# Laying out anew the places of attention steps, q loads and GpSimd sums between the matmul groups of a linear-attention + FFN kernel

## The chip, the cores and the metric

One core of one Trainium2 chip runs the whole program. The time is device microseconds (us) of one execution, lower is better. Engines: PE (TensorE, matmuls), DVE (VectorE), ACT (ScalarE), POOL (GpSimd), and SP, from whose queue nearly all transfers are issued. Each engine runs its own instructions in program order and waits for the others by semaphores.

## The reference

```python
q_s = exp(q - max(q, axis=-1)); q_s /= sum(q_s, axis=-1) + 1e-9     # 8 batches, 8 heads, 576 x 64
k_s = exp(k - max(k, axis=2));  k_s /= sum(k_s, axis=2) + 1e-9      # softmax over the sequence
kv = einsum('bhsd,bhse->bhde', k_s, v)
attn = einsum('bhsd,bhde->bhse', q_s, kv)
x = attn.transpose(0, 2, 1, 3).reshape(4608, 512)
h = x @ w_in                                                        # 512 -> 2048
g = maximum(h, 0) + log1p(exp(-abs(h)))                             # softplus
out = g @ w_out                                                     # 2048 -> 512
```

## The kernel before

The 4608 tokens go in 9 tiles of 512. For each tile the attention gives x (512 tokens x 512), then 16 chunks of the 2048 hidden columns follow, each with an up group of matmuls (x by a chunk of w_in), a softplus, and a down group (by a chunk of w_out). Every f32 product of the FFN is three matmuls on high and low parts (hi/lo, hi/hi, lo/hi). Attention for tile t+1 or later is prepared while the FFN of tile t runs, so PE always has FFN matmuls, and the small attention matmuls (to PSUM tiles `att`) are put between their groups.

The instruction order of every engine is the order of the Python calls, and that order is written out by hand in tables of step names. Tile 0 follows a table `FIRST` that ends at about 119.6 us and is untouched. Tiles 1 and 2 follow `SINGLE`, 32 rows, called **places 0 to 31** here: tile 1 is places 0 to 15, tile 2 is 16 to 31. One row is `before|middle|after`, and the loop runs

```python
ph = up(t, j, cs)                                # 12 matmuls, L758 to L760
before, middle, after = SINGLE[NJ * (t - 1) + place].split("|")
run(before, ops)
split_soft()                                     # g_hi on ACT (L772), g_lo on DVE (L773), for the place before
soft = n, softplus(ph, cs)                       # ACT, L766
run(middle, ops)
while pending and pending[0][0] <= n - 2:
    i, g = pending.pop(0)
    down(*order[i], g)                           # 12 matmuls of two places back, L793 to L795
run(after, ops)
```

Tiles 3 to 8 go in three pairs (3 and 4, 5 and 6, 7 and 8) by `PAIRS[s]`. Each pair has 32 rows `before|after` in which 12, 12, 6 and 12 up matmuls (L1118) come ahead of `before` and 5, 4, 10 and 5 down matmuls (L1138) between `before` and `after`, and then 16 or 18 rows with 12 down matmuls each. Row r of pair s is called P0.0, P0.1 and so on.

The names in a row are steps. A leading digit is the tile that is prepared (in `PAIRS`, `a` and `b` are the two tiles of the next pair). What each step issues:

- `2u30` to `2u35`: the kv product of head pair 3 for tile 2. 0: maximum of k (DVE L418) and its all-reduce over partitions (POOL L420); 2: subtract it (DVE L435); 3: exp in place (ACT L443); 4: reciprocal of the sums (DVE L458, L459); 5: split into hi and lo, ACT L477, ACT L478, DVE L479, twice, one waiting for the other. `2u3*` is the place where the 10 matmuls for it (L448) and the load of a later k/v tile (L375, L376) stand.
- `2x30` to `2x33`: 0 flips softmaxed q into PSUM (DVE L661), 1 stacks its hi and lo parts (ACT L666, DVE L668), `2x3*` is the place of its matmuls (L674), 2 adds the two results (ACT L683, L684, DVE L690, L691), 3 splits x for the FFN. One of these and one `u` share the two PSUM banks `att0` and `att1`.
- `2q0` to `2q11`: softmax of q in halves: 0, 1 maximum (DVE L567), 2 join, 3, 4 subtract (DVE L573), 5, 6 exp (ACT L576), 7, 8 sums (DVE L579), 9 invert, 10, 11 multiply (DVE L587). `2Q0`, `2Q1` load the two halves of q of tile 3 (SP, L542).
- `s40` to `s43`: sums of w_in chunks for the pairs, sum 4 of 8. 0: two additions on POOL (L974), 1: four additions on POOL (L977 to L980), 2: an ACT copy (L984) and a POOL subtraction (L985), 3: the stores (SP). `p4` stores parts (SP), `d0` rearranges kv (ACT, DVE), `h0` splits a chunk of weights.
- `f0` to `f10`: the x operands of the pair by splits (ACT L1006, DVE L1007) and subtractions (DVE L1012); `U`, `D` load weights for the pairs.
- `S2.4`, `J2.4`, `L2.4`, `g1.4`, `G3` in the pairs: ACT copy of a PSUM bank (L1189), DVE addition (L1192), softplus (ACT L1195), and g_hi/g_lo as above.

A softplus and an exp need different tables on ACT; each change of the kind costs an `ACT_TABLE_LOAD`, which stands ahead of the instruction that needs it.

Of the kernel before, what the change touches and what calls it, by code (L numbers as in the profile page):

```python
# [44 lines left out]
SINGLE = [
    "|2u00 2q1 2u10 2u02|",
    "|2u12 2u03 p1 2q0 2q2 h0 2u13 2q4|",
    "2u0* 2q6 2q3 2q8 2u1*|h1|2u20",
    "|2u04 2u30 2u14 2u05 2u15|",
    "s00 p0 2u22 2u32||2q5 2u33",  # L50
    "2q7 2q9 2u23|2u2* 2d0 2u24 2u3* 2q10|2u25 2x00",
    "|s01 2q11|2d1 2u34 2x01 2u35 s02",
    "s03 2d2 2x0* 2x02||2x03 2d3 2x10 2x11 s10",
    "||2x1*",
    "2x12|s11 2x13 s12 p3|s13",
    "2x20 2x21 2x2* 2x22|2x23|2x30",
    "3u00 3u10 2x31||3u12 2Q0",
    "2Q1 3u02 2x3* 2x32 3q1||2x33",
    "3q0 3q2 p2 3u03 3u13 3u0* 3u1* 3u14 3q4 3u04 p4|3q3 3u15|3q5 3u20 3q6 3u30 3u32",
    "||",  # L60
    "3q8 3q7 s20 3u22|3u05 3q9 3u33 3q10 3u23|",
    "3u2* 3u24 3u3*||",
    "3u25 s21 3u34 3x00 3x01|s22 3q11|",
    "3u35|3x0* s23 3x02 3x10|3x11 3Q0",
    "s30 s40 s31||3x1* s50 p7 3x12",
    "3x20 s41||s51",
    "s42 3x21|3x2*|s32 3x22 3x30 s43 s52 3Q1 3x31",
    "4q1||",
    "3x3* 4u00|3x32 4u10 p5 4u02|4u12 4u03",
    "4u13 4u0* 4q0|4u1*|",  # L70
    "s53 p6 4q2 4u04 4q3 4q4 4u20 4u14 4u30 4u22 4q5 4q6|4u32 s33 s60 4u05 4q7 4u33|4q8 4u15 4u23 4q9",
    "||4u2* 4u24 4u3* 4q10 4u34 U0 4u25",
    "4x00|4u35|4x01",
    "4x0* f1 4x02 s70 4x10|s71|",
    "U1 4x11 s72 4q11 4x1* 4x12 4x20||4x21 s61 f0",
    "4x2*||s73 4x22 4x30 s62",
    "s63 4x31|U2 D1 4x3*|4Q0 4Q1 f2 4x32 D0 D2 f4",
]
PAIRS = [
    [  # L80
        "f5 f3 f6 S1.0 J1.0|",
        "|f8 f7 f10 S2.0",
        "au00 f9 S3.0|J3.0",
        "au02 L1.0 J2.0 au10 L4.0 g1.0|aq1 au12",
        "|au03 S1.1 J1.1",
        "|S2.1 au13",
        "L1.1 aq0 au0* aq2 aq4 S3.1 g4.0 au1*|J3.1",
        "|g1.1 aq6 L4.1 L3.0 au14 J2.1",
        "aq3|g4.1 S1.2 J1.2 aq5 au20",
        "|S2.2 L1.2",  # L90
        "au30|au22 S3.2 J3.2",
        "aq7|aq8 au15 aq9 J2.2 L4.2",
        "au04 L3.1 au32 g1.2 g4.2 S1.3 au05 J1.3|",
        "au23 aq10 au2* S2.3 au33 au3* aq11 au24 au34|L1.3 au25 L2.1",
        "S3.3 ax00 J3.3|",
        "ax01 au35 g1.3|J2.3 L4.3 ax0* bu00",
        "ax02 S1.4 ax10|J1.4",
        "|L1.4 aQ0 g4.3 ax11 S2.4 ax1*",
        "ax12|S3.4 J3.4 ax20 g1.4",
        "J2.4 bq0 ax21 L4.4|bu10",  # L100
        "S1.5 J1.5|ax2* L2.0 ax22",
        "L2.2 ax30 g4.4 S2.5 bu02|aQ1",
        "|ax31 S3.5 J3.5 L1.5 ax3* L2.4",
        "bu12 bq1 bq2 bu13 J2.5 L4.5|g1.5 L3.4 bq4 ax32",
        "bu03|S1.6 bu0* g4.5 J1.6 bu1*",
        "bq6|S2.6",
        "bu20 L2.3 bq3 L3.2 bu04|S3.6 L1.6 bu14 J3.6",
        "J2.6|L4.6 g1.6",
        "bq8 S1.7 bu22 bu30|bu23 J1.7 bu32 bq5",
        "|S2.7 bq7 g4.6 bq9",  # L110
        "bu05 bu15 bu33|bu2* S3.7 bu24 J3.7 bq10 bu3*",
        "L1.7 g1.7 bu25 bq11 L3.7 bx00 L4.7 bu34 J2.7|L2.5",
        "g4.7 bx01|G0 bu35",
        "|G1",
        "bx0*|bx02",
        "G2 bx10 L3.6|",
        "nf1|bx11 L3.3 G3 bx1*",
        "G4 nf0|",
        "bx12 bx20 G5|",
        "bx21|bx2*",  # L120
        "nf2 L2.6 L2.7 G6 G7 bx22 L3.5|G8 bx30 bx31",
# [2 lines left out]
        "nf4 G10 bx3*|",
        "bx32|",
        "bQ1 G11 nf5|bQ0 nf3 G12",
        "|nf6 G13 nf8 nf10",
        "nf9 G14 nf7|G15",
    ],
    [  # L130
        "aq0 S1.0|J1.0 aq1 L1.0",
        "S2.0|",
        "S3.0 J3.0|au00",
        "L4.0 au10 au02 J2.0 g1.0|au12 au03",
        "S1.1 J1.1 au13|",
        "g4.0 L1.1 S2.1|",
        "S3.1 aq2 J3.1|",
        "au0* aq3 au1*|J2.1 L3.0 aq4 g1.1 L4.1",
        "S1.2 J1.2 aq6|au14 aq5 au20 g4.1",
        "|au30 S2.2",  # L140
        "|S3.2 au22 J3.2 au23 L2.0",
        "|L4.2 J2.2 L1.2",
        "g1.2 au15 au32 L3.1 S1.3 au33 aq7 aq8 J1.3|au04",
        "|S2.3 au05 g4.2",
        "S3.3 aq9 au2* au3*|aq11 J3.3 bu00 L2.1",
        "L1.3 au34 au24 aq10 au25|g1.3 L4.3 J2.3",
        "bu10 bu12|ax00 au35 g4.3 ax01 ax0* S1.4 J1.4 ax02",
        "ax10 L1.4 S2.4|ax11",
        "S3.4|aQ0 J3.4 bu02 ax1* g1.4",
        "ax12 ax20 bu03 J2.4 L4.4|L2.3",  # L150
        "|ax21 ax2* S1.5 g4.4 J1.5",
        "ax22 bq0 ax30 aQ1|S2.5",
        "ax31|bu13 S3.5 J3.5 ax3* ax32 L1.5 bu0* bq1",
        "|J2.5 L2.4 bu1* bu04 L4.5",
        "bu20 bq2 g1.5 S1.6 bu05 L3.3 bu30|bu32 bq4 bq6 bu22 J1.6",
        "|S2.6 g4.5 L3.4",
        "|S3.6 J3.6 bu14",
        "J2.6|L1.6 g1.6 L4.6",
        "bq3 bu23|L2.5 S1.7 bq8 bu33 g4.6 bq5 J1.7",
        "S2.7 bq7 bu15|bu2* nf0 bq9 bu24 L1.7",  # L160
        "|bu3* bu25 S3.7 J3.7",
        "bq10 bu34 bq11 g1.7 bx00 bu35 J2.7 L4.7|",
        "bx01 g4.7|G0",
        "bx0*|",
        "G1 bx02 L3.2|bx10",
# [1 line left out]
        "|bx11 L3.5",
        "L2.2 G3 bx1* L2.7|bx12",
        "G4 bx20|G5 nf1",
        "bx21|G6 bx2*",  # L170
        "|",
        "G7 bx22 bx30 L3.6 G8|",
        "bQ1 bx31 nf2 G9 nf4|bx3*",
        "bx32|",
        "G10|nf5 L3.7 L2.6 G11",
        "G12 nf6 nf10|",
        "G13 nf3|",
        "G14 nf8|bQ0 nf7 nf9 G15",
    ],
    [  # L180
        "S1.0 J1.0|L1.0",
        "|S2.0",
# [1 line left out]
        "L4.0 J2.0|",
        "g1.0 g4.0 S1.1|J1.1",
        "|S2.1 L1.1",
        "S3.1 J3.1|",
        "L4.1 g1.1|J2.1",
        "S1.2 J1.2|",
        "L1.2|g4.1 S2.2",  # L190
        "S3.2|J3.2",
        "J2.2|L4.2 g1.2",
        "S1.3|J1.3",
        "|S2.3",
        "g4.2 L2.0|S3.3 J3.3",
        "J2.3 L1.3|L3.0 L4.3",
        "g1.3|L2.1 S1.4 J1.4 g4.3",
        "S2.4|",
        "S3.4 J3.4 L1.4|L3.4",
        "|L4.4 J2.4",  # L200
        "g1.4 g4.4|L3.1 S1.5 J1.5 L1.5 L3.3",
        "|S2.5 L3.2",
        "L2.2 S3.5|J3.5",
        "|g1.5 J2.5 L4.5 g4.5",
        "S1.6|J1.6",
        "S2.6|",
        "S3.6 J3.6|",
        "L4.6 L1.6 L2.3 J2.6 g1.6|",
        "S1.7 J1.7 g4.6|",
        "|L2.4 S2.7",  # L210
        "L1.7|S3.7 g1.7 J3.7",
        "|L3.5 L4.7 J2.7",
        "L2.5 g4.7 L2.6|",
        "G0|L2.7",
        "|G1",
        "|G2 G3",
# [1056 lines left out]
```

## Time and profile before

| | |
|---|---|
| median of 3 runs | 853.41 us (851.46 to 854.73) |
| the profiled execution | 854.46 us: its span 852.7 us, and 1.8 us around it |
| mean granted TensorE clock of the span | 0.992 of full |
| busy, share of the span | PE 97%, DVE 64%, ACT 61%, POOL 14% |
| tile 0 (untouched) | 0 to 119.6 us |
| tiles 1 and 2 (`SINGLE`) | 119.6 to 333 us |
| the first two pairs (`PAIRS[0]`, `PAIRS[1]`) | 333 to 646 us |
| the last pair (`PAIRS[2]`) | 646 to 852.7 us |

The profile is of one execution. An engine is busy where it executes; where the text says that an instruction waited, the trace has idle time of its engine just ahead of it and names what ended that time. The granted clock is the share of TensorE's full clock that the chip allowed in a stretch.

### The profile page before, as it was taken

The numbers are of one execution on the slowest core, as the hardware profiler recorded it, in microseconds if no ns is written. First come the engines' busy times: TensorE is split into PE (matmuls) and PEld (weight loads), VectorE is DVE, ScalarE is ACT, GpSimd is POOL, SyncE is SP. The second block draws the span as 40 slices with busy tenths as digits, with TensorE's granted clock in tenths as the row PEclk, the third lists the DMA queues.
The fourth block names the chain that finished last, engine by engine and source line by source line (L and its number), as shares of the span: only waits on it lengthen the run. The fifth ranks groups of instructions, "written<-read, shape, count | busy, mean of one in ns | idle before, by whom it ended". The sixth has DMA issues, their size and how long they took to land.

```text
span 852.7 us, 11505 instructions
## 1 busy us (share of the span) xinstructions
PE 823.4 (97%) x4172; PEld 673.4 (79%) x4172; DVE 543.0 (64%) x849; ACT 519.1 (61%) x861; POOL 115.8 (14%) x203
## 2 busy tenths in 40 slices
...
GB/s 344 371 367 45 40 136 192 81 185 185 126 220 153 269 161 320 216 222 250 169 259 229 236 240 221 202 209 184 198 211 251 174 231 170 232 175 178 119 233 100
DMA packets 79896, 172.72 MB, mean 203 GB/s; under 512 B 5088, under 2 KB 51936, under 8 KB 70624
## 3 DMA queue, kind: packets, MB, share of 16 engines
...
q8 instruction: 33, 0.54, 0.3%
...
## 4 chain that ended last, share of the span: by engine, by line
PE 75%; DVE 9%; ACT 7%; issue 4%; DMA 3%; POOL 2%; SPq 0%; DVEq 0%; ACTq 0%; POOLq 0%
PE po L1138 29%; PE ph L1118 24%; PE ph L758 3%; PE ph L759 3%; PE ph L760 3%; PE po L793 3%; PE po L795 3%; PE po L794 3%; DMA kvt<-in_kv_tail 2%; PE att L674 2%; PE att L448 1%; DVE q L587 1%; DVE g_lo L773 1%; DVE two L668 1%; ACT two L666 1%
## 5 line engine op out<-in xcount | busy, mean ns | idle before, releaser
L1138 PE MATMUL po<-w,g_hi 128*128 128x512 f32 x784 | 246.0, 390 | 0.0
L1118 PE MATMUL ph<-w,w 128*128 128x512 f32 x864 | 213.6, 391 | 0.9 <-ACT x L1189 0.5
L1118 PEld LDWEIGHTS ph<-w,w 128*128 128x128 f32 x864 | 161.0, 188 | 36.2 <-DVE w L1192 1.6
L1138 PEld LDWEIGHTS po<-w,g_hi 128*128 128x128 f32 x784 | 146.7, 188 | 30.4
L1138 PE MATMUL po<-w,g_lo 128*128 128x512 f32 x392 | 152.8, 390 | 0.5 <-DVE g_lo L773 0.5
L1192 DVE TENSOR_TENSOR w<-ph,w 128x512 f32<-128x512 f32 x54 | 37.2, 689 | 90.7 <-PE ph L1118 47.9
L773 DVE TENSOR_TENSOR g_lo<-w,g_hi 128x512 fp32r<-128x512 f32 x77 | 52.8, 690 | 56.3 <-ACT g_hi L772 52.5
L1138 PEld LDWEIGHTS po<-w,g_lo 128*128 128x128 f32 x392 | 73.6, 188 | 16.3 <-DVE g_lo L773 0.9
L772 ACT CAST g_hi<-w 128x512 fp32r<-128x512 f32 x77 | 47.4, 618 | 47.4 <-PE po L1138 45.9
L1189 ACT COPY w<-ph 128x512 f32<-128x512 f32 x54 | 31.7, 587 | 72.9 <-PE ph L1118 72.6
L793 PE MATMUL po<-w,g_hi 128*128 128x512 f32 x164 | 65.3, 398 | 0.0
L795 PE MATMUL po<-w,g_lo 128*128 128x512 f32 x164 | 64.9, 396 | 0.0
L794 PE MATMUL po<-w,g_hi 128*128 128x512 f32 x164 | 64.9, 396 | 0.0
L420 POOL PARTITION_ALL_REDUCE mb<-mx x28 | 28.1, 1003 | 256.5 <-DVE mx L418 236.8
L758 PE MATMUL ph<-x,w 128*128 128x512 f32 x142 | 56.9, 400 | 0.0
L759 PE MATMUL ph<-x,w 128*128 128x512 f32 x142 | 55.5, 391 | 0.0
L760 PE MATMUL ph<-x,w 128*128 128x512 f32 x142 | 55.4, 390 | 0.0
L668 DVE TENSOR_TENSOR two<-att,two 64x512 fp32r<-64x512 f32 x56 | 38.6, 689 | 22.8 <-ACT two L666 22.1
L666 ACT CAST two<-att 64x512 fp32r<-64x512 f32 x56 | 32.6, 581 | 21.9 <-DVE att L661 21.2
L418 DVE TENSOR_REDUCE mx<-kvt 128x128 f32<-128x640 f32 x28 | 36.9, 1329 | 9.9 <-DMA kvt<-in_kv_tail 9.8
L766 ACT ACTIVATE l<-ph 128x512 f32<-128x512 f32 (+1 forms) x50 | 29.1, 581 | 14.9 <-PE ph L760 13.6
L773 DVE TENSOR_TENSOR g_lo<-l,g_hi 128x512 fp32r<-128x512 f32 x46 | 34.1, 741 | 4.8 <-ACT g_hi L772 4.0
...
## 6 DMA issues: line engine op xcount, KB each, us to landing
...
```

Of the source, the lines that this page charges most:

```text
L666: nc.scalar.copy(w[zs, z], ps[zs])
L668: nc.vector.tensor_tensor(out=w[SIDE[1 - z], z], in0=ps[zs], in1=w[zs, z].bitcast(F32), op=ALU.subtract)
L758: nc.tensor.matmul(ph, lhsT=w_hi, rhs=x_hi, start=h == 0, stop=False)
L759: nc.tensor.matmul(ph, lhsT=w_lo, rhs=x_hi, start=False, stop=False)
L760: nc.tensor.matmul(ph, lhsT=w_hi, rhs=x_lo, start=False, stop=h == HP - 1)
L772: copy(g_hi, l)
L773: nc.vector.tensor_tensor(out=g_lo, in0=l, in1=g_hi.bitcast(F32), op=ALU.subtract)
L793: nc.tensor.matmul(po, lhsT=g_hi[:, ms], rhs=w_hi, start=j == chunks(t)[0], stop=False)
L794: nc.tensor.matmul(po, lhsT=g_hi[:, ms], rhs=w_lo, start=False, stop=False)
L795: nc.tensor.matmul(po, lhsT=g_lo[:, ms], rhs=w_hi, start=False, stop=j == chunks(t)[-1])
L1118: nc.tensor.matmul(bank, lhsT=a, rhs=b, start=start and e == k == 0, stop=e == 1 and k == 2, skip_group_check=True)
L1138: nc.tensor.matmul(po, lhsT=g[:, cs], rhs=w, start=first and k == 0, stop=end and k == 2)
```

## The change

Only the strings in `SINGLE` and `PAIRS` differ. Both programs issue the same instructions, with 52 loads of ACT tables in each and the same number of instructions on PE; what differs is between which matmul groups each step stands. Most rows differ, so the diff is cut to five of them (places 2, 5, 20, 25 and P0.0):

```diff
 SINGLE = [
...
-    "2u0* 2q6 2q3 2q8 2u1*|h1|2u20",
...
-    "2q7 2q9 2u23|2u2* 2d0 2u24 2u3* 2q10|2u25 2x00",
...
-    "3x20 s41||s51",
...
-    "s53 p6 4q2 4u04 4q3 4q4 4u20 4u14 4u30 4u22 4q5 4q6|4u32 s33 s60 4u05 4q7 4u33|4q8 4u15 4u23 4q9",
...
+    "2q4 2u0* 2q6 2u04 2q8 2u1*|2u14 h1|",
...
+    "2u23 2d0 2u2* 2q10||2u24 2u15 2u25",
...
+    "|s41 3x1* 3x12|3x20 s50 s42",
...
+    "4u04 4q3 4u14 4u05 4u15 4u20 4q6 4u30 4u22 p6|4q5 s33 4q8|4u23 4u32 4u33 4q7 s53 s60 4q9 U0",
...
 PAIRS = [
...
-        "f5 f3 f6 S1.0 J1.0|",
...
+        "f5 S1.0 f3|f6 J1.0",
...
```

ACT, places 24 to 26, ahead of the kv matmuls `4u2*` and `4u3*`. `kvt` is a k/v tile with its exp in place, `kv_hi00` and `kv_lo00` are the split kv of head pair 0, `q0` and `q1` the halves of q, `l` the softplus result. Before:

```order
L766 ACTIVATE l_2646<-ph1_110 128x512
L477 ACTIVATE kv_hi00_91<-att0_107,r_2623 64x64
L478 ACTIVATE kv_hi00_91<-att0_107,r_2623 64x64
L477 ACTIVATE kv_lo00_99<-att0_107,r_2623 64x64
L478 ACTIVATE kv_lo00_99<-att0_107,r_2623 64x64
L443 ACT_TABLE_LOAD
L443 ACTIVATE kvt_2575<-kvt_2575 128x10x64
L477 ACTIVATE kv_hi01_92<-att1_108,r_2632 64x64
L478 ACTIVATE kv_hi01_92<-att1_108,r_2632 64x64
L477 ACTIVATE kv_lo01_100<-att1_108,r_2632 64x64
L478 ACTIVATE kv_lo01_100<-att1_108,r_2632 64x64
L443 ACTIVATE kvt_2552<-kvt_2552 128x10x64
```

After:

```order
L477 ACTIVATE kv_lo01_100<-att1_108,r_2616 64x64
L478 ACTIVATE kv_lo01_100<-att1_108,r_2616 64x64
L576 ACT_TABLE_LOAD
L576 ACTIVATE q1_2434<-q1_2434 128x1024
L772 CAST g_hi_2649<-l_2570 128x512
L766 ACT_TABLE_LOAD
L766 ACTIVATE l_2653<-ph1_110 128x512
L576 ACT_TABLE_LOAD
L576 ACTIVATE q0_2376<-q0_2376 128x1024
L443 ACTIVATE kvt_2559<-kvt_2559 128x10x64
L443 ACTIVATE kvt_2582<-kvt_2582 128x10x64
```

The eight splits of kv (L477, L478) no longer stand behind the softplus of place 25 and between the two kvt exps, but ahead of it; an exp of q stands ahead of the kvt exps now, which follow each other. (Numbers of buffers differ between the two programs; `kvt_2575` and `kvt_2582` are the same step, `4u33`, as are `kvt_2552` and `kvt_2559`, `4u23`.)

POOL, places 19 to 21, sums 4 (in the tile `spare`) and 5 (in `w2`). Before:

```order
L974 TENSOR_TENSOR w2_2321<-w11_916 128x512
L974 TENSOR_TENSOR w2_2321<-w12_959 128x512
L977 TENSOR_TENSOR spare_2292<-spare_2292 128x256
L978 TENSOR_TENSOR spare_2292<-spare_2292 128x256
L979 TENSOR_TENSOR spare_2292<-spare_2292 128x256
L980 TENSOR_TENSOR spare_2292<-spare_2292 128x256
```

After:

```order
L977 TENSOR_TENSOR spare_2272<-spare_2272 128x256
L978 TENSOR_TENSOR spare_2272<-spare_2272 128x256
L979 TENSOR_TENSOR spare_2272<-spare_2272 128x256
L980 TENSOR_TENSOR spare_2272<-spare_2272 128x256
L974 TENSOR_TENSOR w2_2359<-w11_916 128x512
L974 TENSOR_TENSOR w2_2359<-w12_959 128x512
L985 TENSOR_TENSOR spare_2272<-spare_2272 128x1024
```

The four additions that complete sum 4 now stand ahead of the two first additions of sum 5; the ACT copy of sum 4 (L984) and POOL's L985 need the last of the four (L980).

ACT at the end of place 31 and the start of P0.0, where the first pair begins. `w3`, `w4`, `w5` are the operands `xops[2]`, `xops[3]` and `xops[4]` of the first pair; `x2` is the snapshot of the PSUM bank. Before:

```order
L1006 CAST w4_3030<-x0_2250 128x2x512
L772 CAST g_hi_3033<-l_2994 128x512
L1006 CAST w3_3051<-x0_2250 128x2x512
L1189 COPY x2_3054<-ph0_109 128x512
L1006 CAST w5_3081<-x1_2832 128x2x512
```

After:

```order
L684 COPY l_3014<-att0_107 64x512
L772 CAST g_hi_3033<-l_3000 128x512
L1189 COPY x2_3050<-ph0_109 128x512
L1006 CAST w3_3058<-x0_2266 128x2x512
L1006 CAST w5_3081<-x1_2867 128x2x512
```

The split into `w3` (step `f6`) now stands behind the first snapshot (`S1.0`, L1189), and the split into `w4` further ahead. The matmuls of the second up group of P0 (row P0.1) read `w3`.

## Rows read from the trace of the kernel before

**Rows 1.** The page: span, and busy time of the engines.

```profile
span 852.7 us, 11505 instructions
PE 823.4 (97%) x4172; PEld 673.4 (79%) x4172; DVE 543.0 (64%) x849; ACT 519.1 (61%) x861; POOL 115.8 (14%) x203
```

**Rows 2.** Busy time by stage: window, its length, busy us of each engine, clock.

```profile
core 0: us, PE busy (x) PEld busy (x) DVE busy (x) ACT busy (x) POOL busy (x), PEclk, DMA share, GB/s
119.60:333.00 213.40, 200.91 (x1074) 163.69 (x1072) 156.70 (x243) 138.66 (x235) 88.20 (x120) 0.98 0.54 178
333.00:646.00 313.00, 309.40 (x1569) 253.60 (x1570) 210.56 (x330) 201.97 (x330) 17.15 (x42) 1.00 0.64 226
```

**Rows 3.** Waits of PE, 120 to 333 us: total, times, longest.

```profile
PE att L674 <- DVE two L668: 5.0, 5, 1.9
PE att L448 <- issue: 3.0, 1, 3.0
PE att L674 <- DVE kv_lo L479: 1.7, 2, 1.0
PE att L448 <- ACT kvt L443: 1.2, 2, 1.0
PE att L448 <- POOL x L974: 1.1, 1, 1.1
```

**Rows 4.** Two stretches at a lower granted clock; columns of rows 2.

```profile
166.60:173.50 6.90, 6.18 (x16) 5.05 (x17) 2.76 (x6) 4.30 (x10) 3.25 (x7) 0.51 0.54 182
292.80:296.40 3.60, 3.30 (x42) 3.11 (x43) 3.44 (x9) 3.09 (x6) 1.98 (x2) 0.53 0.08 23
```

**Rows 5.** Timeline of ACT, 148 to 152 us: start, duration, instruction, idle before.

```profile
148.53 1.28 ACT L576 ACT_TABLE_LOAD   x1
149.83 1.06 ACT L576 ACTIVATE q<-q 128x1024 f32<-128x1024 f32 x1
150.79 1.36 ACT L443 ACTIVATE kvt<-kvt 128x640 f32<-128x640 f32 x2
```

**Rows 6.** Timeline, DVE and PE at 164 to 166 us.

```profile
164.48 1.39 DVE L668 TENSOR_TENSOR two<-att,two 64x512 fp32r<-64x512 f32 x2 [1.13 <-ACT two L666]
166.02 0.30 PE L674 MATMUL att<-two,kv_hi 128*128 128x128 f32 x1 [1.30 <-DVE two L668]
```

**Rows 7.** The page: the groups L666 and L418.

```profile
L666 ACT CAST two<-att 64x512 fp32r<-64x512 f32 x56 | 32.6, 581 | 21.9 <-DVE att L661 21.2
L418 DVE TENSOR_REDUCE mx<-kvt 128x128 f32<-128x640 f32 x28 | 36.9, 1329 | 9.9 <-DMA kvt<-in_kv_tail 9.8
```

**Rows 8.** The chain that ended last, at 638 us: 48 down matmuls.

```profile
638.19 10.88 PE po L1138 x48
```

**Rows 9.** Timeline, DVE, ACT and PE at 217 to 293 us (tiles 3 and 4).

```profile
217.13 2.34 DVE L579 TENSOR_REDUCE s<-q 128x32 f32<-128x1024 f32 x2
287.92 0.31 ACT L477 ACTIVATE kv_lo<-att,r 64x64 fp32r<-64x64 f32 x1 [3.49 <-DVE kv_hi L479]
293.10 1.21 PE L448 MATMUL att<-kvt 128*64 128x65 f32 x17 [2.98 <-issue]
```

**Rows 10.** Timeline, ACT, DVE and PE at 253 to 257 us.

```profile
253.14 1.05 ACT L984 CAST spare<-spare 128x1024 fp32r<-128x1024 f32 x1 [2.11 <-POOL spare L980]
256.74 2.18 DVE L773 TENSOR_TENSOR g_lo<-l,g_hi 128x512 fp32r<-128x512 f32 x1
256.85 0.33 PE L674 MATMUL att<-two,kv_hi 128*128 128x192 f32 x1 [1.02 <-DVE two L668]
```

**Rows 11.** Timeline of DVE: the first half of q of tile 4.

```profile
265.09 1.22 DVE L567 TENSOR_REDUCE m<-q 128x32 f32<-128x1024 f32 x1 [1.27 <-DMA q<-in_q]
```

**Rows 12.** Timeline, DVE and PE at 310 to 319 us.

```profile
310.29 3.17 DVE L587 TENSOR_TENSOR q<-q,s 128x1024 f32<-128x1024 f32 x1
318.51 0.36 PE L674 MATMUL att<-two,kv_hi 128*128 128x256 f32 x1 [1.91 <-DVE two L668]
```

**Rows 13.** Timeline, ACT and PE at the start of the first pair.

```profile
331.49 1.05 ACT L1006 CAST w<-x 128x1024 fp32r<-128x1024 f32 x1 [2.27 <-DVE x L1012]
333.08 3.10 PE L1118 MATMUL ph<-w,w 128*128 128x512 f32 x11 [0.50 <-ACT x L1189]
```

More of the change, by code (lines that the diff above doesn't have):

```diff
@@ L60 @@
[L60 to L65, printed above, removed]
-    "3x20 s41||s51",
[L67 to L70, printed above, removed]
-    "s53 p6 4q2 4u04 4q3 4q4 4u20 4u14 4u30 4u22 4q5 4q6|4u32 s33 s60 4u05 4q7 4u33|4q8 4u15 4u23 4q9",
-    "||4u2* 4u24 4u3* 4q10 4u34 U0 4u25",
@@ L73 @@
[L73 to L77, printed above, removed]
+    "2q0|2u00|2u10 2q1 2q2",
+    "|2u02 2q3 2u12 2u03 2u13 p1 h0|2q5",
+    "2q4 2u0* 2q6 2u04 2q8 2u1*|2u14 h1|",
+    "2q7 2u20|2u30 2u05 2u32|",
+    "p0|2u22 2u33 s00 2q9|",
+    "2u23 2d0 2u2* 2q10||2u24 2u15 2u25",
+    "2u3* 2d1 2u34 2x00 2u35 s01 2x01||",
+    "s02 2q11 s03 s10|2x0* p3 2x02 2x03 2x10 s11 2x11|",
@@ new lines @@
+    "||2d2 2x1* 2x12",
+    "2x13 2x20||2Q0",
+    "2x21 s12 2x2* 3u00 s13|2x22|2d3 3u10",
+    "2x23 2x30 2Q1|2x31|",
+    "3q0 3q1|2x3*|3u02 2x32 3u03 3u12 2x33 3u13 3q2 p2",
+    "3u0* 3u04|3u1* 3q4 3u14|3q6 3q3 3q8 3u15",
+    "3u20 3q5 3u30||3q7 3u05 3u32",
+    "|s20 3u22|3u23 3u33 3q9",
+    "p4 3q10 3u2* 3u3*|3q11 3u24 s21 3u34 3u25 3x00|3x01",
+    "|s22|",
+    "||3u35 3x0* s23 3x02 s30 s40 3x10 3x11",
+    "|s31|",
+    "|s41 3x1* 3x12|3x20 s50 s42",
+    "3Q0 3x21 3x2*||s51 s32 3x22 3x30 4q0 p7 s52 4u00 3Q1 3x31 4q1 4q2 4u10",
@@ L78 @@
+    "|4q4|3x3* s43 3x32 4u02",
+    "4u12||p5 4u03",
+    "4u0* 4u13|4u1*|",
+    "4u04 4q3 4u14 4u05 4u15 4u20 4q6 4u30 4u22 p6|4q5 s33 4q8|4u23 4u32 4u33 4q7 s53 s60 4q9 U0",
+    "||4u2* s70 4u24 4q10 4u3* 4u25 4x00",
+    "4u34|4x01 4u35|4q11 s71",
+    "4x0*||",
+    "4x02 4x10 f0 U1 4x11|4x1* 4x12 s72|",
+    "4x20 s61 4x21 f2 4x2*|4x22 4x30|f1 s73 4Q0",
+    "s62 4x31 4x3* f4||4x32 s63 D0 4Q1 D2 U2 D1",
 ]
@@ L80 @@
     [
-        "f5 f3 f6 S1.0 J1.0|",
[L82 to L121, printed above, removed]
-        "|",
-        "G9|",
@@ L124 @@
[L124 to L128, printed above, removed]
-    ],
-    [
[L131 to L165, printed above, removed]
-        "|G2",
[L167 to L170, printed above, removed]
-        "|",
[L172 to L178, printed above, removed]
@@ new lines @@
+        "f5 S1.0 f3|f6 J1.0",
+        "|f8 f7 S2.0",
+        "f10 f9 L1.0 au00 S3.0|J3.0",
+        "L4.0 au02 J2.0 g1.0|",
+        "S1.1 aq1 aq0|J1.1 g4.0",
+        "au03 aq2 au10 S2.1 au12|au13",
+        "S3.1 aq4 au0* J3.1 au1*|",
+        "L3.0 au20 J2.1 L4.1 L1.1 au14 g1.1|",
+        "g4.1 au22 S1.2 aq6 aq3|aq5 J1.2 au04 au30 aq7 aq8",
+        "au32 S2.2|L1.2",
+        "S3.2 aq9 J3.2|g1.2",
+        "au15 L4.2 J2.2|",
+        "au05 S1.3 aq11 J1.3 g4.2|",
+        "au33 aq10 au23 au2* au3*|S2.3 au24 L1.3 au25",
@@ new lines @@
+        "S3.3 ax00|au34 J3.3",
+        "ax01|au35 J2.3 ax0* L4.3",
+        "g1.3 ax02 S1.4|ax10 J1.4",
+        "bu00|L3.1 g4.3 aQ0 ax11 ax1* S2.4",
+        "|S3.4 J3.4",
+        "L1.4 bu10 ax12 ax20|bu12 L4.4 J2.4",
+        "ax21 g1.4|S1.5 g4.4 ax2* J1.5",
+        "ax22 S2.5 L2.0 L2.4|L2.2",
+        "bu02|L1.5 ax30 bq0 S3.5 J3.5 aQ1 ax31 g1.5 bq1",
+        "|J2.5 ax3* bq2 L4.5 L3.2 bu13",
+        "ax32 bu03 bu0*|bq4 S1.6 J1.6 L2.3",
+        "g4.5 S2.6 bq3 L1.6 bu1* bu14|bu20",
+        "|L3.4 bq5 bq7 bu22 bq6 S3.6 g1.6 J3.6",
@@ new lines @@
+        "bu04 L4.6 bu30 L2.1|bq8 J2.6 bu15 bu32",
+        "S1.7 J1.7 g4.6 bu05|",
+        "S2.7 bu23|bu33",
+        "bu2* bq9 L3.3 bq10 S3.7 L2.6 bu3* bu24 L1.7|J3.7 g1.7",
+        "bu25 L4.7 bx00 L3.6 J2.7 bu34|g4.7",
+        "bx01 bu35|G0",
+        "|bq11",
+        "bx0* G1|",
+        "|",
+        "G2 L3.7 bx02 G3 bx10|bx11",
+        "G4 nf0 L3.5|",
+        "bx1*|G5 bx12",
+        "G6 bx20 nf1|",
+        "bx21 L2.5|G7 G8 bx2*",
+        "bx22|nf2",
+        "G9 bx30 nf4 bx31|",
+        "G10|",
```

154 lines of the change are left out of this document (99 added, 55 removed).

## The prediction

> **What bounds the kernel now.** I read the page first: PE is busy for 823.4 us of the span of 852.7 and the next engine, DVE, for 543.0 [rows 1]. The two programs issue the same instructions, so PE's busy time is a floor that the change can't move, except where the clock was low. What it can move is PE's idle time and the stretches at a lower granted clock, and only behind 119.6 us, since tile 0 is untouched. By stage PE is idle for 213.4 - 200.9 = 12.5 us in tiles 1 and 2 and for 313.0 - 309.4 = 3.6 us in the first two pairs [rows 2]. In the last pair no attention is prepared and I expect no change.
>
> The list of PE's waits says what the 12.5 us are: every one is an attention matmul (L448, L674) that comes up in PE's order before its operands are ready [rows 3]. The two at lower clock come right behind such waits: the granted clock was 0.51 from 166.6 to 173.5 us, behind waits of 1.30 [rows 6] and 1.0 us (the longest on kv_lo) [rows 3], and 0.53 behind a wait of 2.98 us [rows 9]. That is the 1.2 GHz level in place of 2.4. Work that took 6.18 us at 0.51 takes 3.2 at full clock, and 3.30 at 0.53 takes 1.75 [rows 4], so the low clock cost 3.0 and 1.6 us. All that the change can win is then 12.5 + 3.6 + 4.6 = 20.7 us, 2.4% of the time.
>
> **The change, wait by wait.** One place of 24 FFN matmuls keeps PE busy for half of 10.88 us, 5.44 [rows 8]: that is what a step gains when it is moved one place ahead of its release.
>
> A, `2u2*` (place 5). ACT does a table load of 1.28, an exp of q of 1.06 and two kvt exps of 1.36 in that order [rows 5], and PE waits 1.0 (the longer of the two on L443 [rows 3]). Now `2q5` stands in place 1, and ACT ends the kvt exps 1.06 us earlier. Gain 1.0, left 0.
>
> B, `2x0*` (place 7). PE waits 1.30 for the stack [rows 6], then 1.0 for kv_lo [rows 3], as `2u35` and `2x01` stand in the same place. Now both stand in place 6, 5.44 us ahead of the release. The work between is two casts of 0.58 [rows 7], two DVE halves of 1.39 together [rows 6], and a split of four ACT pieces of 0.31 [rows 9] with two DVE pieces that I count the same: 1.16 + 1.39 + 1.24 + 0.62 = 4.4 us even with nothing beside anything. Gain 2.3, and with no wait before it the low clock of 3.0 goes too: 5.3.
>
> C, `3u2*` (place 16). The wait of 1.1 that is put down to POOL [rows 3] ends with kvt exps that stood behind a kv split, and DVE came to that split late since place 15 holds two sums of q (2.34 [rows 9]) and much more. Now `3q7` is in place 14, `3q8` in 13, and the splits `3u15`, `3u05` a place earlier. Gain 1.1.
>
> D, `3x0*` to `3x2*` (places 18 to 21): 0.7 (the other one of the two waits on kv_lo that sum to 1.7 [rows 3]), about 0.2, and 1.02 [rows 10]. In the last, ACT stood 2.11 us in L984, the copy of sum 4, for POOL's last addition, and the cast for the stack queued behind it [rows 10]. POOL now does these four additions ahead of sum 5's two large ones, so L984 no longer waits. `3u35` moves only little. I take 1.9 down to 0.5: gain 1.4.
>
> E, place 21, which is new. Ahead of its g_lo DVE now has `4q0`, `4u00`, `3x31`, `4q1`, `4q2`, `4u10`: 1.22 [rows 11] + 1.33 [rows 7] + 1.39 [rows 6] + 1.22 + 1.33 = 6.5 us and the small join, against 5.44 for a place. `4q1` stands close behind the load that it needs (`3Q1`); for its other half DVE waited 1.27 before [rows 11]. The g_lo is not needed until the next place's downs, so from the rows I get a loss of 0 to 2.5 and take 0.5, near the low end because half of place 22's matmuls lie before those downs.
>
> F, `4u2*` (place 26): the largest wait, 2.98 [rows 9]. It is put down to no releaser ("issue"), but ACT shows it: it stood 3.49 us in a kv_lo split for DVE [rows 9], which had maxima ahead of it, and the table load and both exps came behind. Now the splits `4u05`, `4u15` stand ahead of `4u20` and `4u30` on DVE, and behind the softplus of place 25 ACT has 1.28 + 1.06 + 1.36 = 3.7 us to do [rows 5], with half a place and a whole one, 8.16 us, to the release. Left 0.3, gain 2.7, and the low clock of 1.6.
>
> G, from `4x0*` to the first pair: 1.91 [rows 12], 0.50 [rows 13] and about 0.7 in smaller ones, 3.1. The 1.91 comes from `4q11`, which took 3.17 us beside POOL where the same form of operation takes about 1.22 [rows 11, 12]; it is moved to place 27, away from that L985. Gain 1.9 if nothing meets it there, 0 if POOL's additions do; I take 1.4. Against it, `f6` now stands behind `S1.0` on ACT: the second up group of the pair waits for a split of 1.05 on ACT [rows 13] and one on DVE that I count as 1.22, as other operations of 128x1024 [rows 11], with only five downs (1.1) to hide it. The wait there goes from 0.5 to about 1.5. Left 2.4, gain 0.7.
>
> I, the first two pairs: 3.6 [rows 2], spread over waits of about a microsecond and less. Some flips and stacks move ahead of snapshots, others come closer to their release; I take 2.6, gain 1.0.
>
> Sum of the gains: 1.0 + 5.3 + 1.1 + 1.4 - 0.5 + 4.3 + 0.7 + 1.0 = 14.3 us. But 52 releases have been laid anew and I have followed the late ones only. Before, about 20 waited, for 16 us, 0.8 each. I allow six new ones, 5 us, and forecast a gain of 9.2. The span's own execution took 854.46, 1.05 above the median, so I set the gain against the median: 853.4 - 9.2 = **844.2**.
>
> A rule of the Trainium skill speaks against a part of G. Beside POOL's L985 a g_lo took 2.18 us [rows 10] and the division 3.17 [rows 12]; that is all that these rows show. The page "SBUF — State Buffer", section "Who interferes with whom", says that a VectorE instruction with two SBUF inputs and any GpSimd instruction that reads SBUF exclude each other for a whole instruction, and that one with a PSUM input or a single SBUF input is left alone. The trace agrees as far as these two go, both of which read two SBUF tiles. By the rule POOL's additions of sum 7 (`s71`, in place 27 as `4q11` is) can block the division as L985 did, G would gain nothing of the 1.4 and the sum be 12.9; by the rows it is 14.3.
>
> **The rivals.**
>
> 1. The new table makes about as many waits as it removes. For it: six is a guess, every wait removed is one that a profile of the old table named, and a new order has its own. A wait of 1 to 3 us was followed by a low clock at two places, so five waits of 0.85 and two such stretches (4.6) beyond the six already allowed, 8.9 us, cancel the gain. Against it: nothing but E and G looks later in the new order. Time 853.
>
> 2. The other side: POOL's sums land on DVE operations ahead of releases. One hit costs 3.17 - 1.22 = 1.95 us [rows 11, 12]. Such hits would take the place of the six new waits: 14.3 us are used up by seven, and from ten on the kernel is over 0.5% slower. POOL is busy for 88 of the 213 us [rows 2], so the chance to meet is there, but a hit counts only on a chain that ends at PE just then. With ten hits and one stretch of low clock: 853.4 - 14.3 + 19.5 + 3.0 = 861.
>
> 3. The q loads. `Q` steps now stand in the same place as the first maximum that reads them (`3Q1 .. 4q1`, and so in the pairs), and a late load holds DVE, with everything behind it. Before, one held DVE for 1.27 [rows 11], and such a wait in place 21 is in the range of E. If one holds DVE for 6 us there, PE loses some 6, and 3.0 by a low clock behind it: the gain is gone, 853.
>
> **How the numbers follow.** Forecast 0.70, rival 1 0.12, rival 2 0.12, rival 3 0.06. The forecast's own range is 839 (all 14.3, no new waits) to 849. With rivals 1 and 3 the range reaches to 855 on the upper side; below it I go to 838.5, as I may have left too much in I. Out of it stay rival 2 and the tails, less than 2 in 10. A measurement can tell about 0.5% (4.3 us) from no change: faster 0.70, same 0.18, slower 0.12.
>
> **What would show it.** PE's idle time from 119.6 us to the end of the second pair should fall from 16 us to about 11, with no stretch at half clock there. No waits for `2u2*`, `2x0*`, `3u2*`, `4u2*`; L984 of `spare` should start without a wait; a wait of about 1.5 should stand at the second up group of the first pair, and DVE should be late at place 21. Wrong would be: a new wait of over 1.5 us at a release not named here, a stretch of low clock, DVE operations of 128x1024 that take over 2 us ahead of a release, or an idle time in the pairs that grows.

## The result, and the profile after

| | before | changed | ratio, 95% interval |
|---|---|---|---|
| the change timed first | 853.58 us (4 runs) | 842.67 us (4 runs, 839.52 to 843.67) | 0.9869 (0.9835 to 0.9902) |
| once more, other set of runs | 853.86 (9) | 838.79 (5 runs, 836.81 to 841.83) | 0.9818 (0.9794 to 0.9842) |
| a third set | 854.26 (9) | 839.49 (5 runs, 836.79 to 841.76) | 0.9814 (0.9792 to 0.9835) |

The changed kernel is faster by 1.3% in the first set and by 1.8 to 1.9% in the two others; forecast were 844.2 us, a gain of 9.2 and a range that holds all three medians, measured gains of 10.9, 15.1 and 14.8. The profiled execution of the first set took 843.37 us, 11.1 less than that of before. Its page, first the span and the engines:

```profile
span 841.6 us, 11502 instructions
PE 820.4 (97%) x4172; PEld 673.6 (80%) x4172; DVE 543.9 (65%) x849; ACT 518.1 (62%) x861; POOL 109.7 (13%) x203
```

By stage, in the windows of [rows 2] (start, end, length, then busy us of PE, its weight loads, DVE, ACT, POOL, the granted clock, DMA):

```profile
119.60:333.00 213.40, 205.30 (x1102) 167.72 (x1101) 162.41 (x248) 142.51 (x240) 85.79 (x120) 0.98 0.57 189
333.00:646.00 313.00, 313.00 (x1595) 258.62 (x1594) 213.14 (x337) 203.63 (x335) 13.52 (x42) 1.00 0.64 227
```

PE is idle for 213.4 - 205.3 = 8.1 us of the first window (12.5 before) and for nothing that the view shows in the second (3.6 before). The windows don't hold the same work, as the kernel is ahead by then, so here are the pairs from the first matmul of P0.0 to the first of the last pair, before and after:

```profile
328.60:680.20 351.60, 347.58 (x1737) 284.85 (x1736) 242.28 (x369) 225.50 (x366) 17.15 (x42) 1.00 0.64 225
```

```profile
322.90:669.10 346.20, 345.73 (x1737) 285.36 (x1736) 240.54 (x368) 224.56 (x365) 13.52 (x42) 1.00 0.64 228
```

The pairs are 5.4 us shorter: 3.6 of idle time, and 1.9 that the view counts as busy (with the same 1737 matmuls; what these 1.9 are the views don't say). Places 0 to 17 took 114.6 us and now 111.5, places 18 to 31 94.4 and now 91.2. The last pair is the same to 0.1 us, and tile 0 ended 0.6 us later. 3.1 + 3.2 + 5.4 - 0.6 = 11.1.

PE's waits in tiles 1 and 2, total, times and longest, which answer to [rows 3]:

```profile
PE att L674 <- DVE two L668: 5.5, 4, 2.3
PE att L674 <- DVE kv_lo L479: 1.0, 1, 1.0
PE att L448 <- ACT kvt L443: 0.8, 1, 0.8
PE ph L1118 <- DVE w L1007: 0.5, 1, 0.5
PE att L448 <- issue: 0.3, 1, 0.3
```

The long ones of before are gone: `2u2*`, `2x0*`, `4u2*` and `4x2*` don't wait. The 5.5 us on L668 are `2x1*` (2.29), `4x1*` (2.09), `4x3*` (0.6) and `3x2*` (0.6). The first two are new, and behind each the granted clock falls from the 2.4 GHz level to that of 1.2 (0.54 and 0.58 over windows that reach a little past the low stretches), which answers to [rows 4]:

```profile
175.90:179.60 3.70, 3.70 (x12) 3.02 (x12) 2.04 (x5) 1.97 (x4) 0.29 (x2) 0.54 0.34 130
305.30:309.30 4.00, 4.00 (x13) 3.23 (x14) 2.66 (x4) 2.69 (x4) 1.02 (x1) 0.58 0.04 14
```

These stretches cost 3.70 x 0.46 + 4.00 x 0.42 = 3.4 us, where the two of before cost 4.6. The lines that lead to the wait for `2x1*`, of DVE, POOL, SP, ACT and PE, and last the issue of the store with its us to landing:

```profile
165.44 2.89 DVE L773 TENSOR_TENSOR g_lo<-l,g_hi 128x512 fp32r<-128x512 f32 x1
164.53 3.26 POOL L985 TENSOR_TENSOR x<-x 128x1024 fp32r<-128x1024 f32 x1 [1.25 <-ACT x L984]
169.16 0.71 DVE L691 TENSOR_TENSOR att<-att,l 64x512 f32<-64x512 f32 x1
167.75 2.99 POOL L974 TENSOR_TENSOR w<-w 128x512 f32<-128x512 f32 x2
168.23 0.46 SPq L991 DMA_DIRECT2D low<-x  x1
170.84 0.59 ACT L710 CAST x<-att 128x512 fp32r<-128x512 f32 x1 [4.16 <-POOL w L974]
175.68 0.30 PE L674 MATMUL att<-two,kv_hi 128*128 128x128 f32 x1 [2.29 <-DVE two L668]
low<-x SPq DMA_DIRECT2D x1, 256.0 KB, 2.5
```

A g_lo took 2.89 us beside POOL's subtraction of sum 0 in place of 0.69, so the additions of `2x02` behind it (L690, L691) came late, the last at 169.16 + 0.71 = 169.87. ACT's cast of `2x03` stood idle for 4.16 us and began at 170.84, about 1 us after them. For this last us the profile names POOL's L974, but that is of sum 1 and writes another tile; what fits is the store of sum 0 (L991, issued at 168.23, 2.5 us to landing), since `2x03` writes the tile x2 that sum 0 used. This is argued and not shown: L974 ended at 170.74 and the store landed at 170.73. So of the 2.29 us about 1 can lie with the store, and the rest with DVE.

The wait for `4x1*` differs between executions of the same kernel. In this one, and then in the one profiled in the second set:

```profile
295.46 2.54 POOL L974 TENSOR_TENSOR w<-w 128x512 f32<-128x512 f32 x2
296.81 2.27 DVE L587 TENSOR_TENSOR q<-q,s 128x1024 f32<-128x1024 f32 x1
305.27 0.36 PE L674 MATMUL att<-two,kv_hi 128*128 128x256 f32 x1 [2.09 <-DVE two L668]
```

```profile
289.53 2.54 POOL L974 TENSOR_TENSOR w<-w 128x512 f32<-128x512 f32 x2
292.41 1.23 DVE L587 TENSOR_TENSOR q<-q,s 128x1024 f32<-128x1024 f32 x1
299.83 0.36 PE L674 MATMUL att<-two,kv_hi 128*128 128x256 f32 x1 [0.73 <-ACT l L766]
```

In the first, the division `4q11` met POOL's additions of sum 7 and took 2.27 us; in the second POOL was through with them and it took 1.23, and PE waited 0.73.

### The profile page after: what moved, and what is told of

Its sections match the earlier page's. It is cut to its first block, busy times and chain, and to the rows that moved or that the text cites. A ratio compares the mean times of both kernels' runs of the same rounds, so it can differ in the third digit from the quotient of the medians.

```text
span 841.6 us, 11502 instructions
## 1 busy us (share of the span) xinstructions
PE 820.4 (97%) x4172; PEld 673.6 (80%) x4172; DVE 543.9 (65%) x849; ACT 518.1 (62%) x861; POOL 109.7 (13%) x203
## 4 chain that ended last, share of the span: by engine, by line
PE 62%; DVE 2%; DMA 2%; ACT 1%; issue 1%; SPq 0%; DVEq 0%; ACTq 0%
PE po L1138 32%; PE ph L1118 27%; PE att L674 1%; PE att L448 1%; DMA kvt<-in_kv 1%; DMA kvt<-in_kv_tail 1%; ACT w L1006 0%; DVE kvt L435 0%; DVE g_lo L773 0%; PE po L794 0%; PE po L793 0%; DVE s L579 0%; PE po L795 0%; ACT two L666 0%; ACT g_hi L772 0%
## 5 line engine op out<-in xcount | busy, mean ns | idle before, releaser
L1189 ACT COPY w<-ph 128x512 f32<-128x512 f32 x54 | 31.5, 584 | 67.2 <-PE ph L1118 67.1
L420 POOL PARTITION_ALL_REDUCE mb<-mx x28 | 23.2, 830 | 246.1 <-DVE mx L418 223.3
L668 DVE TENSOR_TENSOR two<-att,two 64x512 fp32r<-64x512 f32 x56 | 38.6, 689 | 15.8 <-ACT two L666 14.8
L773 DVE TENSOR_TENSOR g_lo<-l,g_hi 128x512 fp32r<-128x512 f32 x46 | 39.1, 851 | 6.4 <-ACT g_hi L772 5.9
L666 ACT CAST two<-att 64x512 fp32r<-64x512 f32 x56 | 32.5, 580 | 17.5 <-DVE att L661 16.7
L418 DVE TENSOR_REDUCE mx<-kvt 128x128 f32<-128x640 f32 x28 | 37.2, 1330 | 9.2 <-DMA kvt<-in_kv_tail 9.1
```

The costliest lines, as they stand in the source:

```text
L418: nc.vector.tensor_reduce(out=mx, in_=kt.rearrange("p c z d -> p z d c"), op=ALU.max, axis=AX.X)
L668: nc.vector.tensor_tensor(out=w[SIDE[1 - z], z], in0=ps[zs], in1=w[zs, z].bitcast(F32), op=ALU.subtract)
L773: nc.vector.tensor_tensor(out=g_lo, in0=l, in1=g_hi.bitcast(F32), op=ALU.subtract)
```

## The experiments

All were timed beside the kernel before. The first four (new rows of SINGLE alone, of PAIRS alone, of places 0 to 17 only, and the splits of F put back) were on one chip; the others, with the second and third set of the changed kernel, on another.

**The new rows of SINGLE alone, and the new rows of PAIRS alone.** The edits are the two halves of the diff.

> The new rows of SINGLE (tiles 1 and 2) with the old rows of PAIRS. In the profiles of before and of the change, the time from the first up matmul of place 0 to the first of P0.0 fell by 6.3 us and that from there to the first of the last pair by 5.4. My theory: every row acts only on the waits of its own stage, so this kernel keeps the 6.3 and none of the 5.4: 847.3 us against 853.6, PE idle time of 3 to 4 us in the first two pairs as before. Rival: the pairs gained only because tile 2 leaves DVE and ACT with less unfinished work; then the pairs gain here too, and the time is 843 to 844.

> The old rows of SINGLE with the new rows of PAIRS. My theory (stages add up): 853.6 - 5.4 = 848.2 us, with almost no idle time of PE in the first two pairs and the waits of before, 12.5 us, in tiles 1 and 2. Rival (the pairs gain by what tile 2 leaves behind): little gain, 852 to 853. My prediction had priced the pairs at 1.0 us: then 852.6, too.

Measured: 843.67 us, ratio 0.9866 (0.9846 to 0.9886), and 849.79 us, 0.9939 (0.992 to 0.9957), before at 854.84 in this set. The first kernel's waits in the pairs are those of before, the second's are those of the change (the waits of each from P0.0 to the last pair):

```profile
PE att L674 <- DVE two L668: 1.6, 2, 1.0
PE att L674 <- DVE kv_lo L479: 0.7, 1, 0.7
PE ph L1118 <- DVE w L1192: 0.5, 1, 0.5
PE po L1138 <- DVE g_lo L773: 0.5, 1, 0.5
...
```

```profile
PE ph L1118 <- DVE w L1007: 0.5, 1, 0.5
```

So the pairs gain by their own rows, and the rival falls. The product of the two ratios is 0.9866 x 0.9939 = 0.981, which the second and third set measured, on another chip; the first set, at 0.9869, did not. Against my numbers of this experiment the pairs are right (5.1 for 5.4) and SINGLE gave more, 11.2 for 6.3. In its profiled execution the clock stayed at the 2.4 GHz level behind both `2x1*` (2.32) and `4x1*` (2.10), where it fell behind both in the profile that the 6.3 were read from; the last section comes back to this.

**New rows for places 0 to 17 only.** The edit takes the first 18 rows of SINGLE from the change.

> New rows for places 0 to 17 only, the rest as before. By the two profiles these places took 114.6 us before and 111.5 with the change, so 3.1 less: 850.5 us. The profile should have the wait of 2.3 us for 2x1* and the short stretch of low clock behind it, none for 2u2* and 2x0*, and from place 18 on the waits of before (1.02 at 3x2*, 2.98 at 4u2*, 1.91 at 4x2*). Rival: the places behind start earlier and their waits on loads and sums grow by what was won: 853 to 854.

Measured: 850.81 us, 0.9953 (0.9937 to 0.9968), 4.0 us less. The wait for `2x1*` is there (2.31), with low clock behind it, and none for `2u2*` and `2x0*`. From place 18 on the waits of before are there, some in other sizes: 1.85 for `3x0*`, 1.05 for `3x2*`, 1.65 for `4u2*` and 1.94 for `4x2*`; 1.1 at `4x0*` is new. The old rows behind the new ones gave back nothing: this part of the change stands by itself.

**F: the kv splits of place 25 put back.**

```diff
-    "... 4q3 4u14 4u05 4u15 4u20 4q6 4u30 4u22 p6|4q5 s33 4q8|4u23 4u32 4u33 4q7 s53 ...",
+    "... 4q3 4u14 4u20 4q6 4u30 4u22 p6|4u32 s33 4u05 4q5 4u33 4q8|4u15 4u23 4q7 s53 ...",
```

> The changed kernel with the splits 4u05 and 4u15 of place 25 put back behind its softplus, one after 4u32 and one ahead of 4u23, as they stood before; all else as changed. My step F: the order of these splits made the wait of 2.98 us and the low clock of 1.6 us behind it, so the time rises by about 4.3 us, to 847.0, and the wait for 4u2* is back at over 2 us. Rival: the maxima of q and k that now run a few places earlier (4q1, 4q2, 4u10 in place 21, 4q4 in 22) had already taken the load off DVE; then the wait is under 1 us and the time 842.7 to 843.7.

The edit moves a little more than its text says: `4u32` and `4u33` stand further ahead, too, so that the exp of `4u33` comes ahead of the second split and of the exp of `4u23`, as before the change.

Measured: 846.6 us, 0.9906 (0.9888 to 0.9924). By the ratios that is 3 to 8 us more than the changed kernel in its three sets, of which none ran beside it. The wait is back, larger than before, by the same chain (ACT in a kv_lo split for DVE, then PE at `4u2*`), and so is the low clock. The first two lines show what DVE did ahead of the split: two maxima that waited for their k/v loads.

```profile
276.06 1.33 DVE L418 TENSOR_REDUCE mx<-kvt 128x128 f32<-128x640 f32 x1 [2.25 <-DMA kvt<-in_kv_tail]
279.04 1.31 DVE L418 TENSOR_REDUCE mx<-kvt 128x128 f32<-128x640 f32 x1 [1.65 <-DMA kvt<-in_kv_tail]
282.85 0.31 ACT L477 ACTIVATE kv_lo<-att,r 64x64 fp32r<-64x64 f32 x1 [4.32 <-DVE kv_hi L479]
288.97 1.32 PE L448 MATMUL att<-kvt 128*64 128x65 f32 x19 [3.48 <-issue]
288.50:294.60 6.10, 5.63 (x48) 4.87 (x49) 5.89 (x11) 2.92 (x5) 5.48 (x7) 0.50 0.70 217
```

F is shown for these steps together: their order on ACT and DVE is what made the largest wait of the kernel before. In the changed kernel the splits run on DVE ahead of the two maxima, in time that DVE otherwise spends waiting for the loads (2.25 and 1.65 us here, 0.65 and 0.57 there). How much of the 3.48 us comes from the exp of `4u33` (0.73 us on ACT) and not from the splits this run does not tell.

**D: sum 5's first additions ahead of sum 4's last.**

```diff
-    "|s31|",
-    "|s41 3x1* 3x12|3x20 s50 s42",
+    "|s31 s50|",
+    "|s41 3x1* 3x12|3x20 s42",
```

> The changed kernel with s50 (POOL's two first additions of sum 5, 3.05 us) put back ahead of s41, the four that complete sum 4; the ACT copy s42 keeps its new place ahead of 3x21. My step D: the additions of sum 4 end 3 us later, ACT's idle time ahead of that copy rises from 1.0 to about 4 us, the cast for the stack of 3x2* queues behind it, and the wait for 3x2* goes from 0.6 to about 3 us: the time rises by 2.5 us, more with low clock. Rival (the place of s50 on POOL is hidden, the gain of D came from the shorter work on DVE in place 20): the wait stays under 1 us and the time does not change.

Measured: 843.32 us, 0.987 (0.9853 to 0.9888), against 839.49 for the changed kernel beside it: 3.8 us more. ACT's idle time ahead of L984 was 0.72 to 0.99 in the three profiles of the changed kernel, and PE waited 0.3 to 0.6 for `3x2*`; here, with PE behind it, and then the clock:

```profile
250.74 1.05 ACT L984 CAST spare<-spare 128x1024 fp32r<-128x1024 f32 x1 [3.26 <-POOL spare L980]
254.44 0.33 PE L674 MATMUL att<-two,kv_hi 128*128 128x192 f32 x1 [2.91 <-DVE two L668]
255.00:258.90 3.90, 3.90 (x12) 3.05 (x11) 3.51 (x5) 2.68 (x5) 3.90 (x4) 0.56 0.02 4
```

D is shown, and so is how far POOL's order reaches: 3 us of additions on an engine that is busy for 13% of the span, one place too early, end as a wait of PE of 2.9 us, 2.3 to 2.6 more than without.

**Three tries at the waits that are left.** For `2x1*`, sum 0 earlier; for `4x1*`, sum 7 later, or the split f0 behind the release:

```diff
-    "2u23 2d0 2u2* 2q10||2u24 2u15 2u25",
-    "2u3* 2d1 2u34 2x00 2u35 s01 2x01||",
-    "s02 2q11 s03 s10|2x0* ...",
+    "s01 2u23 2d0 2u2* 2q10||2u24 2u15 2u25",
+    "2u3* 2d1 2u34 2x00 2u35 2x01 s02 s03||",
+    "2q11 s10|2x0* ...",
```

```diff
-    "||4u2* s70 4u24 4q10 4u3* 4u25 4x00",
+    "||4u2* 4u24 4q10 4u3* s70 4u25 4x00",
```

```diff
-    "4x02 4x10 f0 U1 4x11|4x1* 4x12 s72|",
+    "4x02 4x10 U1 4x11|4x1* f0 4x12 s72|",
```

> The changed kernel itself once more, beside the three variants of it and on their chip. With the new rows of SINGLE alone the ratio was 0.9866, with those of PAIRS alone 0.9939, with both 0.9869 in another set of runs. If stages add up, this one should be at 0.9866 x 0.9939 = 0.981; if it is at 0.987 again, what the pairs win is given back elsewhere or lies in the spread of the low clock.

> The changed kernel with three steps of sum 0 moved: s01 to the start of place 5, s02 and s03 behind 2x01 in place 6 (they stood in places 6 and 7). Theory: 2x1* waits 2.29 us because 2x03 writes the tile x2, which sum 0 used, and has to wait for the stores s03; the trace puts it down to POOL. The stores now go out about 2 us earlier, so the wait falls to under 0.5 us and the low clock behind it goes: 2 to 3.7 us less than the changed kernel. Rival: it waits for DVE, where a g_lo of 2.89 us beside POOL stands ahead of 2x02; then the wait stays over 1.5 us.

> The changed kernel with s70, the first additions of sum 7 on POOL, moved behind 4u3* in place 26, so that POOL starts them about 3 us later, clear of the division 4q11. Theory (collision on SBUF): 4q11 falls from 2.27 to 1.22 us, the g_lo behind it from 1.23 to 0.69, and the wait of 2.09 for 4x1* to about 0.5: 1.6 us less, up to 3.2 with the low clock. Rival (the split f0 on DVE ahead of the stack makes the wait): the wait stays at 2 us.

> The changed kernel with the split f0 moved from ahead of 4x11 to behind 4x1*. f0 takes 1.23 us on DVE just ahead of the stack, but the stack's cast on ACT ends only 0.03 us before DVE is through. Theory (collision): DVE was late already at the flip, f0 hides behind ACT's two casts for half of it, and the wait for 4x1* falls by 0.6 only, to 1.5. Rival (f0 makes the wait): it falls by 1.23 or more, to 0.9 or less.

Measured: the changed kernel 838.79 us, 0.9818, as the stages add up to; sum 0 early 840.31, 0.9835 (0.9814 to 0.9857); sum 7 later 839.84, 0.9827 (0.9806 to 0.9847); f0 later 842.38, 0.9863 (0.9842 to 0.9883). The first two make no difference that these runs can tell, the third is slower by 3.6 us, with intervals that just meet.

Sum 0 early missed: the wait for `2x1*` stayed at 2.33, and a down group waited 0.82 for the first g_lo below. But neither theory had it whole. The store no longer ended the wait (ACT's cast of `2x03` now stood for DVE's additions); POOL, now about 2 us earlier, was beside three DVE operations in a row:

```profile
163.38 2.54 DVE L773 TENSOR_TENSOR g_lo<-l,g_hi 128x512 fp32r<-128x512 f32 x1 [0.21 <-ACT g_hi L772]
165.84 2.31 DVE L587 TENSOR_TENSOR q<-q,s 128x1024 f32<-128x1024 f32 x1
168.06 1.77 DVE L773 TENSOR_TENSOR g_lo<-l,g_hi 128x512 fp32r<-128x512 f32 x1
```

For `4x1*` the pair says less than I wanted. Both variants waited about 0.75 there, but so did the changed kernel beside them (0.73), because `4q11` met no addition in that execution. So neither theory on `4x1*` was tested. With f0 later `4x3*` waited 2.87 in place of 1.12, by a collision that the next pair of kernels shows more closely.

**Both causes of the wait for `2x1*` at once,** and then with sum 7 later and f6 first. The first edit is sum 0 early and

```diff
-    "2q11 s10|2x0* p3 2x02 2x03 2x10 s11 2x11|",
-    "||2d2 2x1* 2x12",
-    "2x13 2x20||2Q0",
+    "2q11|2x0* p3 2x02 2x03 2x10 2x11|",
+    "||2d2 2x1* s10 2x12",
+    "2x13 s11 2x20||2Q0",
```

the second has besides it the edit to s70 above and, in `PAIRS[0]`,

```diff
-        "f5 S1.0 f3|f6 J1.0",
+        "f5 f6 S1.0 f3|J1.0",
```

> The changed kernel once more, as the measure for the three beside it: ratio 0.982 to 0.987 as in the two sets so far.

> The changed kernel with sum 0 early (s01 in place 5, s02 and s03 in place 6) and the additions of sum 1 later (s10 behind 2x1*, s11 in place 9). Moving sum 0 alone left the wait for 2x1* at 2.34 us, but the stores no longer ended it: three DVE operations beside POOL took 2.54, 2.31 and 1.77 us in place of 0.69, 1.22 and 0.69. Theory (two causes, one behind the other): with POOL's large additions of sum 1 gone from that stretch only the first is hit, DVE is through 2 us earlier, the stores have landed, and the wait falls to under 0.4 us: 2 us less than the changed kernel, more where the low clock came behind it. Rival: a third cause stands behind these two, and the wait stays above 1 us.

> As f1_sums01_apart, and s70 behind 4u3*, and in the first pair f6 ahead of S1.0 on ACT as before the change. Theory: f6 behind S1.0 is what the wait of 0.48 us at the second up group comes from, so that wait goes or moves to S1.0 (0.5 before the change); with the other two 2.0 to 3 us less than the changed kernel, 836 to 838 where that is at 839 to 840. Rival: the waits that stay (4u0*, 4x1*, 4x3*) grow by what is won at 2x1*, and the time is that of the changed kernel.

Measured: the changed kernel 839.49 us, 0.9814; the first 839.78, 0.9822 (0.98 to 0.9844); the second 838.72, 0.9814 (0.9797 to 0.9831). The wait for `2x1*` is gone in both: the view names none there. So the places of sums 0 and 1 on POOL together are its cause. Moving sum 0 alone did not do; sum 1 alone was not tried, so that the store of sum 0 has a part in it stays argued. The time did not follow, and the rival of the second kernel holds: other waits took up what was won. A down group waits 0.8 for its g_lo in both, as with sum 0 early. In the first `4x3*` now waits 3.42 us, and its lines stand beside those of the changed kernel in the second set, where it waited 1.12:

```profile
310.50 2.38 POOL L985 TENSOR_TENSOR w<-w 128x1024 fp32r<-128x1024 f32 x1 [1.16 <-ACT w L984]
310.98 2.99 DVE L1007 TENSOR_TENSOR w<-x,w 128x1024 fp32r<-128x1024 f32 x1
315.52 0.41 PE L674 MATMUL att<-two,kv_hi 128*128 128x256 f32 x1 [3.42 <-DVE two L668]
```

```profile
310.63 1.23 DVE L1007 TENSOR_TENSOR w<-x,w 128x1024 fp32r<-128x1024 f32 x1
310.86 3.23 POOL L985 TENSOR_TENSOR w<-w 128x1024 fp32r<-128x1024 f32 x1 [1.16 <-ACT w L984]
```

In the changed kernel the split of step f1 (L1007) began 0.23 us ahead of POOL's subtraction, kept its 1.23 us, and POOL took 3.23 for 2.4. Here POOL was first by 0.48 us, and the split took 2.99; with f0 later POOL was first by 0.46 and it took 3.02. In the second kernel the split kept clear, `4u0*` waited 1.57 (0.7 and 1.35 in the changed kernel), and f6 first turned the wait of 0.47 at the second up group into 0.67 at a later one. No variant beat the changed kernel by more than the noise.

## Why the prediction was right, and where its sizes were off

The direction and its ground hold: PE's busy time is the floor, the change moved waits and low clock, and the waits that I named went. That the total came so near is in part luck. Without I and with the allowance the forecast for places 0 to 31 was a gain of 8.2 us, and the first profile has 6.3; for the pairs it was 1.0, and the profile has 5.4. The second and third set gained more than the 14.3 that I had for no new waits at all. (The tables have 56 releases and not 52: 24 in SINGLE and 16 in each of the first two pairs.) Several of my signs of being wrong showed, too: new waits of over 1.5 us at `2x1*` and `4x1*`, a low clock behind both, and a division of 2.27 us ahead of a release; and L984 of `spare` still waited 0.99. Step by step:

- A and C held: `2u2*` has no wait, `3u2*` 0.3 for 1.1. (In C only `3u05` moved a place ahead; `3u15` is in place 13 in both tables.)
- B was right for `2x0*`, whose 2.3 us and low clock of 3.0 went, and wrong as a gain of 5.3: 2.3 + 1.7 came back one release later at `2x1*`, which had not waited before. In part this can be that PE was held up at `2x0*` first; the order of sums 0 and 1 against DVE is in it, as the experiments show. The allowance for new waits, 5 us, holds this: with 0.5 more at `4u0*` (0.76 for 0.28) it was 4.5.
- D was priced at 1.4: 1.9 became 1.6 in the first profile and 0.3 to 0.4 in the two others. The order of POOL's additions alone is worth 2.3 to 2.6 us of wait and with the clock 3.8 us of time, since L984 stands ahead of the stack's cast on ACT.
- E did not come: no down group of places 21 and 22 waits for its g_lo (the 0.6 at `3x2*` in place 21 is D's). I took 0.5 for a DVE that has more than a place's work there; the matmuls ahead of the next downs covered all of it.
- F held in kind (a wait of 2.98 to none). Undone, it costs 3 to 8 us, which does not tell whether my 4.3 was too little.
- G: its own terms (0.5 + 1.5 + 0.7) leave 2.7 us and not the 2.4 that I wrote, a gain of 0.4. Measured are 3.2 in the first profile and 2.3 in the second. The wait on f6 was 0.47 and not 1.5: I had let the snapshot S1.0 begin at the end of the 12 up matmuls, but it reads the bank of the first six only, and began 1.5 us after the first matmul (322.9 and 324.4), not 2.7. But the division was not clear of POOL in place 27. That it would be clear of POOL once it was away from L985 failed: it took 2.27 us beside L974. The page "SBUF — State Buffer" of the Trainium skill, section "Who interferes with whom", says that a VectorE instruction with two SBUF inputs contends with a GpSimd instruction that reads SBUF; the trace agrees in this execution (2.27 us beside L974, 1.23 us in the second set clear of it). For a single SBUF input the page excepts instructions in a 2-port mode, which my sentence on it left out.
- I is the term that was mis-sized: 1.0 forecast, 5.4 measured, and 5.1 in the kernel with the new PAIRS rows alone. I had not followed the pairs' rows release by release and had left 2.6 us of waits there; in the profile of the change the view names none from the second up group to the end of the second pair. By the windows DVE and ACT are busy for under 70% of the pairs, so there is room for nearly every step to stand ahead of its release; which of the moved steps did it was not tested.

Rival 1 (as many new waits) came true for places 0 to 31 in part: 8.1 us of waits in the first profile, of which 4.9 are new (`2x1*`, `4x1*` and 0.5 at `4u0*`). Rival 2's collisions are real, up to 2.2 us each, but did not decide. Rival 3 did not show: in tiles 1 and 2 and the first two pairs DVE waited 1.6 us in all for loads of q, and 2.3 before.
